# A decode kernel's last 30 microseconds: reordered tail products, residual accumulated in PSUM, and a different way of storing the result

## The chip, the cores and the metric

One core of one Trainium2 chip. The metric is the device time of one execution in microseconds (us); in this study the fast runs of one kernel on one chip lay at most 0.17% apart (front_longer, 661.01 to 662.14). The kernel before took 660.36 us (median of 3 runs, 660.25 to 660.48). The span of a profile is about 1.3 us shorter than the time of the same run.

## The reference, cut to what matters

A decoder block for one new token and two batch rows: layer norm, attention over a cache of 8192 positions with 32 heads, output product, residual, a second layer norm, a gated ReLU network, residual.

```python
x = A_x                                            # [2, 1, 512]
h  = x + attention(layernorm(x), k_cache, v_cache, wq, wo)   # caches [2, 32, 8192, 128] bf16
n  = layernorm(h)
h2 = h + (relu(n @ W_gate) * (n @ W_up)) @ W_down  # 512 -> 1376 -> 512
```

The caches are 2 x 134 MB, read once. The result is 2 x 512 bf16 values, 2 KB.

## The kernel before

The kernel streams K and V tiles of 4 MB through four SBUF slots. For each of 32 pairs of heads, VectorE computes three quarters of the scores, TensorE one quarter ("K part"), ScalarE the exponentials, TensorE the V product. The last two pairs, P0 and P1, are written out after the loop. The product with `wo` is spread: most of it (`L463`, 30 matmuls) can be done as soon as the third-last pair's result is gathered. This is TensorE's order at the end:

```python
k_part(tail, P0, (2, 3, 4, 5), ((k2p, 1),))          # scores of P0
nc.tensor.wait_ge(l2p, 1)
o_gather(tail)
nc.tensor.wait_ge(a2p, 7)                            # ScalarE copied the gathered O_all
nc.tensor.wait_ge(sem_wo, 16)
for r in range(DR):                                  # "wo product", 30 matmuls in four column tiles
    i = nc.tensor.matmul(Op[1][32 * (r % 4):32 * (r % 4) + B, :], lhsT=O_all[:, r, :], rhs=X[:, r * D:(r + 1) * D], ...)
tail.mark("op", i)
nc.tensor.wait_ge(a2p, 9)                            # ScalarE copied it to os_sb
for c in range(DC):                                  # "little product into W", fp32
    nc.tensor.matmul(Wp[:, c * B:(c + 1) * B], lhsT=os_sb[:]..., rhs=sel2[:], ...)
k_part(tail, P1, (10, 11, 12, 13), ((k2p, 2),))      # scores of P1
pv(tail, P0, ...)                                    # V product of P0
pv(tail, P1, ((V_LAST, J, (sem_vl[0] ...)), (0, V_LAST, (sem_vl[1] ...))), ...)   # of P1, by two loads
```

After that: `O_cur` (the last pair normalised), its product with wo, `hb` (the residual h), the mean, `d_b` (h minus its mean), the up and gate products, `hd` (their gated product), the down product. The down product is accumulated in four column tiles of one PSUM bank: columns 128m to 128m+127 of the result stand on partitions 32m and 32m+1. The ending before:

```python
for m in range(4):
    i = nc.tensor.matmul(Op[0][32 * m:32 * m + B, 0:128], lhsT=hd[0:kp, f * B:(f + 1) * B], rhs=wdn_block[:, 128 * m:128 * m + 128], ...)
t_y = pe.run(i)
dve.last()
dve.wait(t_y)
t = dve.run(nc.vector.scalar_tensor_tensor(          # one operation on 128 partitions: y * r2 + h
    out=o_r, in0=Op[0][:, 0:128], scalar=r2[:, 0:1], in1=h_r, op0=ALU.mult, op1=ALU.add))
sp.wait(t); act.wait(t)
for b, e in enumerate((nc.sync, nc.scalar)):         # four rows of 256 bytes each, from partitions b, b+32, b+64, b+96
    e.dma_start(out[b, 0].rearrange("(k n) -> k n", n=128), o_r[b:128:32, :]).then_inc(sem_out, 16)
nc.sync.wait_ge(sem_out, 16 * B)
```

The softmax here doesn't subtract the row's maximum and nothing guards it: scores larger than these inputs give would overflow.

## Time and profile before

| what | before |
|---|---|
| time | 660.36 us |
| span of the profiled run | 659.2 us |
| read from HBM | 281 MB at 426 GB/s over the span |
| last V tile landed, its two loads | 643.40 and 645.88 us |
| W_gate landed | 652.51 us |
| last rows of W_down landed | 656.06 us |
| last matmul ends | 656.70 us |
| stores issued, last store landed | 657.23, 659.14 us |

The landings are the moments at which a load's semaphore gets its last increment in the trace.

From the page of the kernel before: the rows by slice (40 slices of 16.5 us; a digit is tenths of DMA or clock, where PEclk is the granted clock, the share of TensorE's full speed that the chip allowed), and the line of the chain of waits by engine (the work that ended last, followed back from the end).

```profile
PEclk9856556565756657555665756756555765655656
DMA  8999999999999999999999999999999999999997
GB/s 366 444 437 431 420 445 416 443 428 431 438 422 441 422 439 433 428 435 424 441 422 439 433 428 433 426 441 422 439 434 426 435 424 441 424 437 433 428 417 295
...
DMA 76%; DVE 19%; PE 4%; issue 1%; ACT 1%; SPq 0%; DVEq 0%
```

The DMA engines are busy for 90% or more (digit 9) from the second slice to the last but one, so the kernel is a stream of 281 MB with a start and an end. How a landing is read: the issue of the last load, from SyncE's row of the timeline (start, length), and its line in the DMA issues of the page, which ends with the time from issue to landing:

```profile
628.22 2.39 SPq L706 DMA_DIRECT2D wd_last<-in_B_W_down_dram  x1
...
wd_last<-in_B_W_down_dram SPq DMA_DIRECT2D x1, 96.0 KB, 27.8
```

628.22 + 27.8 gives 656.0 us. Most of the chain's 4% of TensorE (some 26 us) lies before that, from 628 us on, beside the last loads. The timeline of the kernel before, from the wo product on; columns are start, busy time, engine, line, operation, in brackets the idle time before it and its releaser; SPq and ACTq are the DMA queues of SyncE and ScalarE, on which a store is issued:

```profile
628.78 3.58 PE L463 MATMUL O<-X,O_all 128*2 128x512 bf16 x30 [0.33 <-ACT O_all L671]
632.40 0.60 ACT L677 ACTIVATE os_sb<-O 128x512 f32<-128x512 f32 x1 [2.89 <-PE O L463]
633.05 2.03 PE L469 MATMUL W<-sel,os_sb 128*128 128x2 f32 x8 [0.69 <-ACT os_sb L677]
641.05 6.08 PE L405 MATMUL O<-slot,e 128*16 128x512 bf16 x56
647.38 0.61 PE L405 MATMUL O<-slot,e 128*16 128x512 bf16 x8
649.86 0.16 DVE L510 TENSOR_TENSOR O_cur<-Ob,zi 128x4 bf16<-128x4 f32 x1 [1.99 <-PE Ob L417]
653.29 1.72 PE L756 MATMUL O<-d_b,slot 128*128 128x2 bf16 x44
656.38 0.32 PE L808 MATMUL O<-wd_last,hd 96*2 96x128 bf16 x4
656.85 0.35 DVE L815 SCALAR_TENSOR_TENSOR kT<-O,r,kT 128x128 bf16<-128x128 f32 x1 [1.27 <-PE O L808]
657.22 0.65 SPq L820 DMA_DIRECT2D out_dram<-kT  x1
657.23 0.61 ACTq L820 DMA_DIRECT2D out_dram<-kT  x1
```

No V product and no gate product waits for a DMA here: V's last part starts at 647.38 us, 1.5 us after its data. In this trace compute is a little behind the stream. The chain of waits (start, us, what; "issue" is time for which the profile shows no wait) says the same: its end is compute, one exchange after the other.

```profile
655.36 1.37 PE O L808 x23
656.74 0.03 issue
656.76 0.02 DVEq L32
656.78 0.06 issue
656.85 0.35 DVE kT L815
```

### The profile page before, as it was taken

What the parts mean: (1) busy time and instruction counts of PE and PEld (TensorE: products, weight loads), DVE (VectorE), ACT (ScalarE), POOL (GpSimd) and SP (SyncE); (2) the same over time, 40 slices, a digit from 0 to 9 for tenths busy, and PEclk for the clock granted to TensorE, in tenths of its full rate; (3) what the DMA queues carried; (4) which work ended last, traced back from release to release, by engine and by line L of the source; (5) the groups of instructions that cost most, each with busy time, mean ns of one, the idle gap of its engine ahead of it and who ended that gap; (6) DMA issues with size and microseconds to landing.
All of it is one profiled execution on the core that took longest, in us unless ns stands there. A gap on an engine that the chain in (4) does not pass through costs nothing.

```text
span 659.2 us, 7582 instructions
## 1 busy us (share of the span) xinstructions
PE 324.3 (49%) x3073; PEld 188.6 (29%) x3073; DVE 469.2 (71%) x280; ACT 213.6 (32%) x431; POOL 73.5 (11%) x125
## 2 busy tenths in 40 slices
PE   2753454435455343655535364443556444354577
PEld 0331332213233121433313142221324222133344
DVE  1585576788767678776768877676886767787991
ACT  1622333143342223334223343422324332333250
POOL 3002002020200202020020201002020110202000
PEclk9856556565756657555665756756555765655656
DMA  8999999999999999999999999999999999999997
GB/s 366 444 437 431 420 445 416 443 428 431 438 422 441 422 439 433 428 435 424 441 422 439 433 428 433 426 441 422 439 434 426 435 424 441 424 437 433 428 417 295
DMA packets 10653, 281.17 MB, mean 427 GB/s; under 512 B 1202, under 2 KB 1300, under 8 KB 1812
## 3 DMA queue, kind: packets, MB, share of 16 engines
q1 hardware_dynamic: 10632, 281.06, 99.3%
q8 instruction: 5, 0.08, 0.1%
q14 instruction: 4, 0.03, 0.0%
q10 hardware_dynamic: 12, 0.00, 0.0%
HBM read 281.05 MB, written 0.00 MB: 426 GB/s over the span
## 4 chain that ended last, share of the span: by engine, by line
DMA 76%; DVE 19%; PE 4%; issue 1%; ACT 1%; SPq 0%; DVEq 0%
DMA slot<-in_A_k_cache_dram 76%; DVE prod L540 16%; DVE prod L549 2%; PE O L405 1%; PE O L463 1%; PE T L381 0%; ACT kT L566 0%; PE W L469 0%; DVE scores L554 0%; PE S L756 0%; PE O L756 0%; PE O L808 0%; PE Ob L417 0%; SPq L172 0%; PE S L364 0%
## 5 line engine op out<-in xcount | busy, mean ns | idle before, releaser
L540 DVE TENSOR_TENSOR prod<-slot,q_c 128x12288 bf16<-128x12288 bf16 x32 | 209.9, 6558 | 148.0 <-DMA slot<-in_A_k_cache_dram 141.3
L405 PE MATMUL O<-slot,e 128*16 128x512 bf16 x1024 | 119.3, 621 | 219.9 <-ACT e L495 146.2
L549 DVE TENSOR_TENSOR prod<-prod 128x6144 bf16<-128x6144 bf16 (+3 forms) x128 | 212.2, 1657 | 7.8
L566 ACT ACTIVATE kT<-T 128x1024 bf16<-128x1024 bf16 x128 | 126.1, 1022 | 144.6 <-PE T L381 141.9
L381 PE MATMUL T<-ident_f,slot 128*128 128x128 f32 x512 | 108.6, 365 | 29.1 <-DVEq L587 29.1
L405 PEld LDWEIGHTS O<-slot,e 128*16 128x16 bf16 x1024 | 26.4, 114 | 287.0 <-ACT e L495 172.9
L495 ACT ACTIVATE e<-scores 64x96 bf16<-64x96 f32 x64 | 19.5, 304 | 239.6 <-DVEq L601 238.9
L381 PEld LDWEIGHTS T<-ident_f,slot 128*128 128x128 f32 x512 | 79.0, 188 | 44.2 <-DVEq L587 43.3
L537 POOL COPY q_c<-q_all 128x136 bf16<-128x136 bf16 x32 | 57.2, 1788 | 195.5 <-DVEq L591 152.5
L364 PE MATMUL S<-q_c,kT 128*128 128x4 bf16 x1024 | 47.4, 168 | 40.8 <-ACT kT L566 40.0
L364 PEld LDWEIGHTS S<-q_c,kT 128*128 128x128 bf16 x1024 | 39.1, 104 | 67.9 <-ACT kT L566 66.8
L417 PE MATMUL Ob<-sel,os_sb 128*128 128x4 f32 x136 | 30.1, 345 | 24.2 <-ACT os_sb L569 24.2
L417 PEld LDWEIGHTS Ob<-sel,os_sb 128*128 128x128 f32 x136 | 28.6, 311 | 26.1 <-ACT os_sb L569 26.1
L520 POOL MEMSET O_l<- 128x40 bf16 (+1 forms) x13 | 1.8, 136 | 303.9 <-DVEq L598 303.9
L554 DVE TENSOR_REDUCE scores<-prod 128x96 f32<-128x768 bf16 x32 | 30.5, 953 | 2.8
L566 ACT ACT_TABLE_LOAD x15 | 19.2, 1283 | 0.3
L495 ACT ACTIVATE e<-S 64x32 bf16<-64x32 f32 x64 | 13.0, 202 | 15.1 <-PE S L364 14.7
L569 ACT ACTIVATE os_sb<-O 128x512 f32<-128x512 f32 x17 | 10.1, 597 | 12.8 <-PE O L405 12.4
L495 ACT ACTIVATION_READ_ACCUMULATOR e<-S 64x1 f32 x64 | 12.8, 201 | 0.7
L495 ACT ACTIVATION_READ_ACCUMULATOR e<-scores 64x1 f32 x64 | 11.8, 185 | 0.0
L426 PEld LDWEIGHTS Ob<-zs,ones_f 128*128 128x128 f32 x30 | 7.1, 296 | 12.5 <-issue 12.5
L525 POOL COPY rsel<-rows 128x30 bf16<-128x30 bf16 x28 | 5.9, 209 | 33.3 <-DVEq L598 32.5
(104 smaller groups left out, 90.6 us busy)
## 6 DMA issues: line engine op xcount, KB each, us to landing
slot<-in_A_k_cache_dram SPq DMA_DIRECT2D x32, 4096.0 KB, 32.1
slot<-in_A_v_cache_dram SPq DMA_DIRECT2D x31, 4096.0 KB, 30.3
slot<-in_A_wq_dram SPq DMA_DIRECT2D x1, 4096.0 KB, 12.2
X<-in_A_wo_dram SPq DMA_DIRECT2D x1, 3840.0 KB, 45.8
slot<-in_A_v_cache_dram SPq DMA_DIRECT2D x1, 3072.0 KB, 23.3
slot<-in_B_W_up_dram SPq DMA_DIRECT2D x1, 1376.0 KB, 23.2
slot<-in_B_W_gate_dram SPq DMA_DIRECT2D x1, 1376.0 KB, 26.2
slot<-in_A_v_cache_dram SPq DMA_DIRECT2D x1, 1024.0 KB, 25.4
```

Of the source, the lines that this page charges most:

```text
L364: i = nc.tensor.matmul(Sp[p % 2][:, 2 * jj:2 * jj + 4], lhsT=kv_[:, k, r, :], rhs=q_c[p % 2][:, 4 * r:4 * r + 4], start=(r == 0), stop=(r ...
L381: i = nc.tensor.transpose(Tp[g % 2][:, k * 128:(k + 1) * 128], k_t[:, j:j + 2, :].rearrange("p j d -> p (j d)").bitcast(F32), ident_f[:])
L405: i = nc.tensor.matmul(Op[0][c:c + 16, :], lhsT=e_t[q][:, j // VJ, :], rhs=v_t[:, j:j + VJ, :].rearrange("p j d -> p (j d)"), start=(q == ...
L417: i = nc.tensor.matmul(Ob[:, 0:4], lhsT=os_sb[:, jj * Dh:(jj + 1) * Dh], rhs=sel[:, 4 * jj:4 * jj + 4], start=(jj == 0), stop=(jj == VJ - 1))
L426: return nc.tensor.matmul(bank[:, ZC:ZC + 8], lhsT=ones_f[:], rhs=zs[:], start=True, stop=True)
L495: i = nc.scalar.activation(out=e_t[q][h, j0 // VJ:j1 // VJ, 8 * q:8 * q + 8].rearrange("p g (j a) -> p g j a", a=2)[:, :, :, a], in_=src(h ...
L537: nc.gpsimd.tensor_copy(out=q_c[p % 2][:], in_=q_all[:, p]).then_inc(g2d, 1)
L540: return nc.vector.tensor_tensor(out=prod[:, 0:JC, :], in0=tile((2 * p) % 4)[:, 0:JC, :], in1=q_c[p % 2][:, 8:QW].unsqueeze(1).broadcast_t ...
L549: run(nc.vector.tensor_tensor(out=prod[:, 0:JC, 0:w], in0=prod[:, 0:JC, 0:w], in1=prod[:, 0:JC, w:2 * w], op=ALU.add))
L554: return nc.vector.tensor_reduce(out=scores[p % PG][:, 0:JC], in_=prod[:, 0:JC, 0:8], axis=AX.X, op=ALU.add)
L566: to_pe(nc.scalar.activation(out=kT[gg % 2][:], in_=Tp[gg % 2][:].bitcast(BF16), func=ACT.Copy))
L569: to_pe(nc.scalar.activation(out=os_sb[:], in_=Op[0][:], func=ACT.Copy))
```

## The change

In a few words: the last product stays in four column tiles; VectorE and ScalarE copy two tiles each to two neighbouring partitions; two stores of 512-byte rows. The diff does more than that. It (a) puts the last K part before the wo product and the little product into W between the two V products; (b) accumulates the residual on TensorE and moves the layer norm's reciprocal to the up branch, so that nothing but copies remains at the end; and (c) changes copies and stores. The core of it:

```diff
@@ (a) TensorE's order; ScalarE's order follows it
                 k_part(tail, P0, (2, 3, 4, 5), ((k2p, 1),))
+                k_part(tail, P1, (7, 8, 9, 10), ((k2p, 2),))
                 nc.tensor.wait_ge(l2p, 1)
                 o_gather(tail)
                 ... wo product ...
                 tail.mark("op", i)
-                nc.tensor.wait_ge(a2p, 9)
+                pv(tail, P0, ((JC, J, ((slot_sem[1], 16),)), (0, JC, ((a2p, 13),))))
+                nc.tensor.wait_ge(a2p, 14)
                 ... little product into W ...
-                k_part(tail, P1, (10, 11, 12, 13), ((k2p, 2),))
-                pv(tail, P0, ((JC, J, ((slot_sem[1], 16), (a2p, 6))), (0, JC, ((a2p, 8),))))
                 pv(tail, P1, ...)
@@ (b) residual into the down product's bank; variance before gate; scale on u
-                        i = nc.tensor.matmul(
-                            Tp[0][32 * k:32 * k + B, c:128:DC], lhsT=hb[...], rhs=ident[...], start=True, stop=True)
+                        nc.tensor.matmul(
+                            Op[0][32 * k:32 * k + B, c:128:DC], lhsT=hb[...], rhs=ident[...],
+                            start=(c == 0), stop=False, skip_group_check=True)
+                for k in range(2):
+                    i = nc.tensor.matmul(Sp[0][:, 32:32 + B], lhsT=onesn[:], rhs=vh[:, k * B:(k + 1) * B], ...)
                 t_g = ffn_in(Op[1], wgt, 0, FC)
-                dve.run(nc.vector.tensor_copy(out=u_sb[:], in_=Sp[1][:, 0:FC * B]))
-                dve.run(nc.vector.tensor_copy(out=h_r, in_=Tp[0][:, 0:128]))
+                dve.run(nc.vector.tensor_tensor(out=u_sb..., in0=Sp[1]..., in1=r2... , op=ALU.mult))
@@ (c) the ending
-                dve.last()
-                t = dve.run(nc.vector.scalar_tensor_tensor(
-                    out=o_r, in0=Op[0][:, 0:128], scalar=r2[:, 0:1], in1=h_r, op0=ALU.mult, op1=ALU.add))
-                for b, e in enumerate((nc.sync, nc.scalar)):
-                    e.dma_start(out[b, 0].rearrange("(k n) -> k n", n=128), o_r[b:128:32, :])...
+                for m in range(2):
+                    dve.run(nc.vector.tensor_copy(out=o_r[:, 128 * m:128 * m + 128], in_=Op[0][32 * m:32 * m + B, 0:128]))
+                for m in range(2, 4):
+                    act.run(nc.scalar.activation(out=o_r[:, 128 * m:128 * m + 128], in_=Op[0][32 * m:32 * m + B, 0:128], func=ACT.Copy))
+                for m, (e, r) in enumerate(((sp, dve), (act, act))):
+                    e.wait((r.sem, r.count))
+                    e.eng.dma_start(out[:, 0, 256 * m:256 * m + 256], o_r[:, 256 * m:256 * m + 256])...
```

`o_r` is now two neighbouring partitions of 512 columns.

More of the change, by code (lines that the diff above doesn't have):

```diff
@@ L141, in bass_sequential_preLN__gqa_block_cached__glu_gated_reglu__decode_kernel @@
         vr = sb("vr", [128, B], F32)
-        ve = sb("ve", [128, 1], F32)
-        r2 = sb("r2", [128, 1], F32)
-        h_r = kT[0][:].bitcast(F32)[:, 0:128]
-        o_r = kT[1][:, 0:128]
+        ve = sb("ve", [128, B], F32)
+        r2 = sb("r2", [128, B], F32)
+        o_r = kT[1][0:B, 0:D]
         vh = sb("vh", [128, 2 * B], BF16)
@@ L457, in program @@
                 k_part(tail, P0, (2, 3, 4, 5), ((k2p, 1),))
+                k_part(tail, P1, (7, 8, 9, 10), ((k2p, 2),))
                 nc.tensor.wait_ge(l2p, 1)
                 o_gather(tail)
-                nc.tensor.wait_ge(a2p, 7)
+                nc.tensor.wait_ge(a2p, 12)
                 nc.tensor.wait_ge(sem_wo, 16)
@@ L669, in program @@
                         evacs()
+                    elif p == P1:
+                        evacs()
                         act.wait(tok("og", NI))
@@ L673, in program @@
                             in_=Op[1][:, 0:B * DR].rearrange("p (b r) -> p b r", r=DR), func=ACT.Copy))
-                        act.wait(t_s[p])
-                        exp_dve(p)
+                        act.wait(t_s[P0])
+                        exp_dve(P0)
                         act.wait(tok("op", NI))
                         to_pe(nc.scalar.activation(out=os_sb[:], in_=Op[1][:], func=ACT.Copy))
-                    elif p == P1:
-                        evacs()
                         act.wait(t_s[p])
@@ L766, in program @@
                     for c in range(DC):
-                        i = nc.tensor.matmul(
-                            Tp[0][32 * k:32 * k + B, c:128:DC], lhsT=hb[:, c * B:(c + 1) * B],
-                            rhs=ident[:, 32 * k:32 * k + 32], start=True, stop=True)
-                t_hr = pe.run(i)
-                pe.wait((sem_w[1], 16))
-                t_g = ffn_in(Op[1], wgt, 0, FC)
+                        nc.tensor.matmul(
+                            Op[0][32 * k:32 * k + B, c:128:DC], lhsT=hb[:, c * B:(c + 1) * B],
+                            rhs=ident[:, 32 * k:32 * k + 32], start=(c == 0), stop=False, skip_group_check=True)
                 dve.last()
@@ L782, in program @@
                 t_vh = dve.run(nc.vector.tensor_tensor(out=vh[:, B:], in0=vr[:], in1=vh[:, 0:B], op=ALU.subtract))
+                pe.wait(t_vh)
+                for k in range(2):
+                    i = nc.tensor.matmul(Sp[0][:, 32:32 + B], lhsT=onesn[:], rhs=vh[:, k * B:(k + 1) * B],
+                                         start=(k == 0), stop=(k == 1))
+                t_var = pe.run(i)
+                pe.wait((sem_w[1], 16))
+                t_g = ffn_in(Op[1], wgt, 0, FC)
+                dve.wait(t_var)
+                dve.run(nc.vector.tensor_scalar_add(out=ve[:], in0=Sp[0][:, 32:32 + B], scalar1=eps))
+                dve.last()
+                dve.run(nc.vector.reciprocal(out=r2[:], in_=ve[:]))
+                dve.last()
                 dve.wait(t_u)
-                dve.run(nc.vector.tensor_copy(out=u_sb[:], in_=Sp[1][:, 0:FC * B]))
-                dve.wait(t_hr)
-                dve.run(nc.vector.tensor_copy(out=h_r, in_=Tp[0][:, 0:128]))
+                dve.run(nc.vector.tensor_tensor(
+                    out=u_sb[:].rearrange("p (f b) -> p f b", b=B),
+                    in0=Sp[1][:, 0:FC * B].rearrange("p (f b) -> p f b", b=B),
+                    in1=r2[:].unsqueeze(1).broadcast_to([128, FC, B]), op=ALU.mult))
                 dve.last()
@@ L791, in program @@
                     in1=u_sb[:], op0=ALU.max, op1=ALU.mult))
-                pe.wait(t_vh)
-                for m in range(4):
-                    for k in range(2):
-                        i = nc.tensor.matmul(Sp[0][32 * m:32 * m + B, 32:33], lhsT=vh[:, k * B:(k + 1) * B],
-                                             rhs=onesn[:, 0:1], start=(k == 0), stop=(k == 1))
-                t_var = pe.run(i)
-                dve.wait(t_var)
-                dve.run(nc.vector.tensor_scalar_add(out=ve[:], in0=Sp[0][:, 32:33], scalar1=eps))
-                dve.last()
-                dve.run(nc.vector.reciprocal(out=r2[:], in_=ve[:]))
                 pe.wait(t_hd)
@@ L810, in program @@
                             rhs=(wdn[:, f, :] if f < 10 else wd_last[:])[:, 128 * m:128 * m + 128],
-                            start=(n == 0), stop=(n == FC - 1))
+                            start=False, stop=(n == FC - 1), skip_group_check=True)
                 t_y = pe.run(i)
-                dve.last()
                 dve.wait(t_y)
-                t = dve.run(nc.vector.scalar_tensor_tensor(
-                    out=o_r, in0=Op[0][:, 0:128], scalar=r2[:, 0:1], in1=h_r, op0=ALU.mult, op1=ALU.add))
-                sp.wait(t)
-                act.wait(t)
-                for b, e in enumerate((nc.sync, nc.scalar)):
-                    e.dma_start(
-                        out[b, 0].rearrange("(k n) -> k n", n=128), o_r[b:128:32, :]).then_inc(sem_out, 16)
+                act.wait(t_y)
+                for m in range(2):
+                    dve.run(nc.vector.tensor_copy(
+                        out=o_r[:, 128 * m:128 * m + 128], in_=Op[0][32 * m:32 * m + B, 0:128]))
+                for m in range(2, 4):
+                    act.run(nc.scalar.activation(
+                        out=o_r[:, 128 * m:128 * m + 128], in_=Op[0][32 * m:32 * m + B, 0:128], func=ACT.Copy))
+                for m, (e, r) in enumerate(((sp, dve), (act, act))):
+                    e.wait((r.sem, r.count))
+                    e.eng.dma_start(out[:, 0, 256 * m:256 * m + 256], o_r[:, 256 * m:256 * m + 256]).then_inc(sem_out, 16)
                 nc.sync.wait_ge(sem_out, 16 * B)
```

## The prediction

> **What bounds it now.** The DMA engines. The page's slices show 417 to 445 GB/s from the second to the last but one; 281 MB pass in a span of 659.2 us. The chain of waits is 76% DMA, all cache loads. The loads queue without a gap to the end. Landings by the trace (issue plus time to landing): last V tile 643.40 and 645.88 us, W_up 649.19, W_gate 652.51, W_down blocks 653.78, 655.08, 655.86, its last rows 656.06. Only 3.1 us come after the last input byte. All that the diff moves runs after 620 us.
>
> **What the diff does**, more than its title says:
>
> (a) From 628 us TensorE does the last K part (6.0 us) before, not after, the product with wo (3.6); the little product into W (2.0) goes between the two last V products (3.4 and 2.6 until the z sum). Nothing is removed. TensorE is the chain here by the timeline: from 628.1 to 647.0 it has 18 us of matmuls and 0.95 us of gaps for two ScalarE copies. In the new order: K part 628.05 to 634.1; the gathered copy waits behind the two exponentials of that K part (0.85 us), so wo runs 635.3 to 638.9; V to 642.3; W to 644.4; scores and V tile are there at 643.4; last V to 647.0. The same end within 0.2 us: a gap for a gap.
>
> (b) The layer norm's reciprocal goes onto the up branch, the residual is accumulated on TensorE. The variance matmuls (0.2 us, hidden so far behind the wait for hd) now stand between up and gate, two instead of eight: +0.1 us on the chain. VectorE is done with scaling about 654.1, before gate ends at 655.1.
>
> (c) Tail. One VectorE operation of 0.35 us (128x128 from PSUM) becomes two copies on VectorE and two on ScalarE. A 128-column copy took VectorE 0.29 us; two overlapping: estimate 0.43. ScalarE took 0.20 us for 32 columns, 0.60 for 512: estimate 0.28 for 128, 0.57 for two. Fewer partitions save nothing: columns set the time. So ScalarE's store is issued 0.2 us later. Stores: now two of four 256-byte packets. [...] Here a 256-byte packet takes 15 ns; the 1.9 us from issue to last landing are 1.25 to 1.5 until the first packet and 0.35 of receipt. So 512-byte rows save at most 0.1 us.
>
> **Sum.** (a) 0.0, (b) +0.1, (c) +0.2 less at most 0.1: +0.2 us on 660.36. A gain is capped: the last W_down rows land at 656.06, where the down product ends at 656.74 now, so (a) and (b) could give 0.6 us at most.
>
> Predicted 660.6 us, range 659.6 to 661.8. Faster by over 2%: 0.005; within: 0.985; slower: 0.01.
>
> **What would show it.** Landings unmoved within 0.2 us. TensorE starting its last stretch at 628 us and O_cur normalised at 649.9 within 0.3; order K, wo, V, W, V. Gate ending about 655.1, down about 656.8. ScalarE copies of 0.28 us, VectorE copies of 0.2 to 0.3; the ScalarE store issued about 657.6; last landing about 659.3.
>
> **What would make it wrong.** The granted clock: 0.5 nearly throughout the end, with one full grant at 646.9 to 650.4 us, under which the eight fp32 matmuls of the collection take 1.07 us; at half clock they took 1.87. If the new order moves that grant, the end moves by up to 1 us either way. Also a ScalarE table load before the new copies (1.28 us), which I don't expect.

The sum is 0.0 + 0.1 + 0.2 - 0.1 = +0.2 us. The -0.1 is the author's estimate, and the trace of the kernel before bounds it: the data packets of a store take 15 to 16 ns each, the first ones begin 1.25 and 1.51 us after the issues, and from a queue's first packet to the end of its last it is 0.07 and 0.08 us, so fewer packets can save no more than that if the time before the first stays. "Receipt" is the stretch from the last packet to the last landing (0.32 us from its end at 658.82 to 659.14). That fewer partitions save nothing was not shown by a trace at that time; the runs show it for a copy of 128 columns on VectorE: 0.29 us on 128 partitions (old_store), 0.28 on two (the changed kernel). The table loads of the kernel before, 1283 ns in the mean, all lie before 575 us, and the changed kernel has none before its new copies either.

## The result, and the profile after

The changed kernel took 660.12 us (median of 6 runs, 659.90 to 660.32) beside 660.34 us of the kernel before (6 runs, 660.09 to 660.49). The ratio is 0.9996, with a 95% interval of 0.9984 to 1.0009: the same, within 2% and within the noise of the ratio. (A ratio is the mean time of one kernel's fast runs over that of the other's of the same rounds, so it is not quite the ratio of the medians quoted.) Five more rounds on another chip gave 659.96 beside 660.52 us, ratio 0.9992 (0.9979 to 1.0006). So the medians were 0.2 and 0.6 us apart. The ratios alone do not show a gain; the traces below do, step by step.

The same timeline of the changed kernel:

```profile
636.01 3.41 PE L463 MATMUL O<-X,O_all 128*2 128x512 bf16 x30 [1.09 <-ACT O_all L672]
638.96 2.19 PE L404 MATMUL O<-slot,e 128*16 128x512 bf16 x32
641.08 2.03 PE L470 MATMUL W<-sel,os_sb 128*128 128x2 f32 x8
643.55 1.47 PE L404 MATMUL O<-slot,e 128*16 128x512 bf16 x24 [0.45 <-DMA slot<-in_A_v_cache_dram]
646.13 0.61 PE L404 MATMUL O<-slot,e 128*16 128x512 bf16 x8 [0.78 <-DMA slot<-in_A_v_cache_dram]
648.60 0.16 DVE L509 TENSOR_TENSOR O_cur<-Ob,zi 128x4 bf16<-128x4 f32 x1 [2.84 <-PE Ob L416]
652.68 1.72 PE L755 MATMUL O<-d_b,slot 128*128 128x2 bf16 x44 [0.45 <-DMA slot<-in_B_W_gate_dram]
656.34 0.28 PE L807 MATMUL O<-wd_last,hd 96*2 96x128 bf16 x4
656.67 0.57 ACT L818 ACTIVATE kT<-O 2x128 bf16<-2x128 f32 x2 [9.29 <-PE O L807]
656.67 0.59 DVE L815 CAST kT<-O 2x128 bf16<-2x128 f32 x2 [1.97 <-PE O L807]
657.27 0.26 ACTq L822 DMA_DIRECT2D out_dram<-kT  x1
657.29 0.31 SPq L822 DMA_DIRECT2D out_dram<-kT  x1
```

The last load, in the same two views of the changed kernel:

```profile
630.22 0.50 SPq L705 DMA_DIRECT2D wd_last<-in_B_W_down_dram  x1
...
wd_last<-in_B_W_down_dram SPq DMA_DIRECT2D x1, 96.0 KB, 26.1
```

It was issued 2 us later and landed at 656.3 us all the same, since it stands at the end of a queue that keeps the engines busy (the DMA row has a 9 to the last slice but one in both traces). Three things differ in the timeline. O_cur comes 1.26 us earlier (648.60 against 649.86). That lead is gone by the end: both V parts and the gate product now wait for their data, and the last matmul ends at 656.62 us where it ended at 656.70. And the ending has other pieces: two copies one after the other on each engine (0.57 and 0.59 us in all), and stores whose issue takes 0.26 and 0.31 us instead of 0.61 and 0.65.

The chain of waits now ends with the landing of the last W_down block, then the work that follows it:

```profile
629.40 26.68 DMA slot<-in_B_W_down_dram
656.09 0.04 issue
656.13 0.52 PE O L807 x7
656.65 0.02 issue
656.67 0.28 DVE kT L815
656.95 0.03 issue
656.98 0.28 DVE kT L815
```

The stores themselves are seen in the waits of SyncE's queue, the line for its wait on the stores' semaphore (total us, times, longest). First the kernel before:

```profile
SPq L822 <- DMA out_dram<-kT: 1.3, 1, 1.3
```

and the changed kernel:

```profile
SPq L823 <- DMA out_dram<-kT: 1.0, 1, 1.0
```

This wait starts when the issue is over. With the issue time added, a store takes 1.9 us before and 1.3 us after. The span splits as follows, up to rounding, by the records of the two traces:

| stretch | before | after | difference |
|---|---|---|---|
| start to last W_down landing | 656.06 | 656.29 | +0.23 |
| last landing to end of the last matmul | 0.64 | 0.33 | -0.31 |
| last matmul to issue of the later store | 0.52 | 0.67 | +0.15 |
| issue to last landing of the stores | 1.92 | 1.28 | -0.63 |
| landing to end | 0.03 | 0.03 | 0.00 |
| span | 659.17 | 658.61 | -0.56 |

The first row is the stream's own variation: over all full-size traces the last W_down landing lay between 655.99 and 656.36 us, with no order to it. The third row has two parts: the copies take 0.59 us where one operation took 0.35, but they start 0.05 us after the last matmul where it started after 0.15. The diff also drops a wait of VectorE before it (`dve.last()`, which the chain before shows as DVEq L32). The other rows are the subject of the experiments.

### The profile page after: what moved, and what is told of

It reads as the page before. It is cut to its first block, busy times and chain, and to the rows that moved or that the text cites. A ratio compares the mean times of both kernels' runs of the same rounds, so it can differ in the third digit from the quotient of the medians.

```text
span 658.6 us, 7569 instructions
## 1 busy us (share of the span) xinstructions
PE 326.1 (50%) x3066; PEld 192.1 (29%) x3067; DVE 469.4 (71%) x280; ACT 214.2 (33%) x433; POOL 72.7 (11%) x125
## 4 chain that ended last, share of the span: by engine, by line
DMA 80%; DVE 18%; issue 1%; SPq 0%; DVEq 0%; PE 0%
DMA slot<-in_A_k_cache_dram 76%; DVE prod L539 16%; DMA slot<-in_B_W_down_dram 4%; DVE prod L548 2%; DVE scores L553 0%; SPq L171 0%; SPq L702 0%; SPq L698 0%; DVE kT L815 0%; DVEq L586 0%; PE O L807 0%; DVEq L590 0%; SPq L175 0%; SPq L174 0%; DVE zi L505 0%
## 5 line engine op out<-in xcount | busy, mean ns | idle before, releaser
L404 PE MATMUL O<-slot,e 128*16 128x512 bf16 x1024 | 117.2, 609 | 219.3 <-ACT e L494 146.3
L380 PE MATMUL T<-ident_f,slot 128*128 128x128 f32 x512 | 112.8, 376 | 29.4 <-DVEq L586 29.4
L380 PEld LDWEIGHTS T<-ident_f,slot 128*128 128x128 f32 x512 | 81.9, 193 | 44.4 <-DVEq L586 43.6
L565 ACT ACT_TABLE_LOAD x15 | 19.2, 1283 | 0.3
```

What stands on the lines that cost most here:

```text
L380: i = nc.tensor.transpose(Tp[g % 2][:, k * 128:(k + 1) * 128], k_t[:, j:j + 2, :].rearrange("p j d -> p (j d)").bitcast(F32), ident_f[:])
L404: i = nc.tensor.matmul(Op[0][c:c + 16, :], lhsT=e_t[q][:, j // VJ, :], rhs=v_t[:, j:j + VJ, :].rearrange("p j d -> p (j d)"), start=(q == ...
L565: to_pe(nc.scalar.activation(out=kT[gg % 2][:], in_=Tp[gg % 2][:].bitcast(BF16), func=ACT.Copy))
```

## The experiments

Twelve kernels ran, in three groups; each group shared its own runs of the kernel before. Times are medians. "Matmul to end" is the end of the last matmul to the end of the span, "issue to landing" that of the later store, both from the trace.

The theory after the result was: the ending (c) gives the gain, the order (a) brings the front forward but the landings hold it back. The rival was that the order gives the gain.

### after_again: the changed kernel once more, no edit

> The changed kernel once more, as the control for its chip. Every theory: 0.2 to 0.3 us under the kernel before. Theory G (the gain of 0.2 us is the ending: the stores save 0.6 us from issue to landing, the copies cost 0.25): the down product's last matmul to the end of the span takes 1.9 to 2.0 us whatever the granted clock does, and the last W_down landing is at 656.0 to 656.4. Rival H (the new order gains, the front is earlier by 1.2 us): O_cur normalised at 648.6 again. If the front's 1.2 us came from the granted clock instead, it lies anywhere between 648.5 and 650 and moves with the clock records of 630 to 650 us.

Measured: 659.96 us beside 660.52. Matmul to end 1.98 us, last landing 656.01, O_cur 648.44. The ending repeats to 0.01 us. O_cur also repeats, so this run by itself does not tell order from clock.

### old_store: the changed kernel with the old copy and the old stores

```diff
-                for m in range(2): ... dve copies ...; for m in range(2, 4): ... act copies ...
-                ... two stores of two 512-byte rows ...
+                t = dve.run(nc.vector.tensor_copy(out=o_w, in_=Op[0][:, 0:128]))        # 128x128
+                for b, e in enumerate((nc.sync, nc.scalar)):
+                    e.dma_start(out[b, 0].rearrange("(k n) -> k n", n=128), o_w[b:128:32, :])...
```

> The changed kernel with the ending before: one VectorE copy of 128x128 from PSUM, two stores of four 256-byte rows from four partitions each. Theory G: copy 0.29 us in place of 0.60, each store's issue 0.6 us long again, first packet 1.25 us after issue, last landing 1.9 us after it; from the last matmul to the end 2.3 us, so 0.3 us over the changed kernel and equal to the kernel before. Rival H (the order gives the gain): stays 0.2 us under the kernel before.

Measured: 660.06 us (changed kernel 659.96, before 660.52, same chip). The copy:

```profile
656.58 0.29 DVE L814 CAST kT<-O 128x128 bf16<-128x128 f32 x1 [1.79 <-PE O L808]
```

Issue to landing 1.84 us, matmul to end 2.25 us, which is 0.26 us over the changed kernel, as theory G expected of the trace. The expected time, "equal to the kernel before", was missed: it lay 0.1 us over the changed kernel. The single copy here is 0.29 us faster up to the issue than the changed kernel's four (0.38 against 0.67), and the stores lose 0.56 us. Against the kernel before, the store is issued 0.14 us sooner (0.38 against 0.52): the old ending on top of (b) has a lighter operation (0.29 us for 0.35) and no `dve.last()`. So the new stores and copies by themselves are worth 0.26 us in the trace, and some of the shorter ending comes with (b).

### split_rows: the changed kernel, each 512-byte row as two pieces of 256

```diff
-        o_r = kT[1][0:B, 0:D]
+        o_p = kT[1][0:B, 0:640].rearrange("p (m n) -> p m n", n=160)[:, :, 0:128]      # gaps between the pieces
...
+                    e.eng.dma_start(out[:, 0, 256 * m:256 * m + 256].rearrange("b (k n) -> b k n", n=128),
+                                    o_p[:, 2 * m:2 * m + 2, :])...
```

> The changed kernel with each 512-byte row of a store cut into two pieces of 256 bytes (padded apart in SBUF), still from two partitions. If the size of the rows under 512 bytes or the number of packets makes the store slow (rival R): issue to last landing about 1.9 us, as before. If the spread over four partitions does (theory P): about 1.3 us, as in the changed kernel. The time differs from the changed kernel by +0.6 us under R, 0 under P.

Measured: 659.71 us, issue to landing 1.29 us, matmul to end 1.99 us. The trace has eight packets of 256 bytes, as the kernel before has, of 15 to 18 ns each, where the changed kernel has four of 512 bytes, of 27 to 32 ns. Rival R falls: neither the row size nor the number of packets made the old store slow. The issue lines of this run:

```profile
657.11 0.27 ACTq L822 DMA_DIRECT2D out_dram<-kT  x1
657.14 0.32 SPq L822 DMA_DIRECT2D out_dram<-kT  x1
```

### four_adjacent and two_strided: number of partitions, or their distance?

Both give a wrong result: they store from the wrong partitions. Both start from old_store.

```diff
 # four_adjacent: four 256-byte rows per store, from neighbouring partitions
-    o_w[b:128:32, :]
+    o_w[4 * b:4 * b + 4, :]
 # two_strided: two 512-byte rows per store, from partitions b and b + 32
-    out[b, 0].rearrange("(k n) -> k n", n=128), o_w[b:128:32, :]
+    out[b, 0].rearrange("(k n) -> k n", n=256), o_w[b:64:32, :]        # o_w now 256 columns wide
```

> Ending as in old_store, but the four 256-byte rows of each store come from four neighbouring partitions, not from every 32nd (wrong result on purpose). If the distance of 32 partitions makes the store's issue long (theory N): issue 0.3 us, last landing 1.3 us after issue. If the number of partitions, four against two, does (theory M): issue 0.6 us, landing 1.8 to 1.9 us.

> Ending as in old_store, but each store takes two 512-byte rows from two partitions 32 apart (wrong result on purpose: half of each row is old data). Theory N: issue 0.6 us, landing 1.8 to 1.9 us after it. Theory M: issue 0.3, landing 1.3.

Measured, one look each: four_adjacent 1.33 us from issue to landing, two_strided 1.87 us. The issue lines, first four_adjacent:

```profile
656.68 0.32 SPq L818 DMA_DIRECT2D out_dram<-kT  x1
656.69 0.28 ACTq L818 DMA_DIRECT2D out_dram<-kT  x1
```

then two_strided:

```profile
657.05 0.63 SPq L818 DMA_DIRECT2D out_dram<-kT  x1
657.05 0.60 ACTq L818 DMA_DIRECT2D out_dram<-kT  x1
```

Theory N holds and M falls: it is the distance of 32 partitions, not the count, that doubles the issue (0.28 to 0.32 us against 0.60 to 0.63). The first packet follows it: 0.73 to 0.76 us after the first issue with neighbouring partitions, 1.23 to 1.25 with partitions 32 apart. Four rows of 256 bytes from neighbouring partitions are nearly as quick as two of 512 (1.33 against 1.28 us). Only distances of 1 and 32 were tried; whether 2 or 16 would do the same, and why the distance costs time, stays open.

### one_store: one store of two 1024-byte rows

```diff
-                for m, (e, r) in enumerate(((sp, dve), (act, act))): ... two stores ...
+                sp.wait((dve.sem, dve.count), (act.sem, act.count))
+                nc.sync.dma_start(out[:, 0, :], o_r).then_inc(sem_out, 16)
+                nc.sync.wait_ge(sem_out, 16)
```

> The changed kernel with one store on SyncE alone, two rows of 1024 bytes. If two stores issued at the same time hold each other up (rival Q): issue to last landing 1.2 us or less, 0.1 to 0.2 us shorter than with two. If each store's cost is its own (theory P): 1.3 us, no difference in time.

Measured: 659.72 us (659.46 to 659.99) beside 659.96 of the changed kernel and 660.52 of the kernel before; correct. Issue to landing 1.14 us, matmul to end 1.86 us. With two stores the landings come in two pairs 0.17 to 0.18 us apart (658.38/658.39 and 658.56/658.58 in the changed kernel); with one store there is one pair. Rival Q is right about the size, 0.14 us; that the rows of one store are also longer (1024 bytes) was not tested apart. This is the best correct version found; its lead over the changed kernel is seen in the trace, and the ratio (0.9989, 0.9976 to 1.0003) does not resolve it.

### order_only and old_order: the order (a) alone, and everything but the order

order_only is the kernel before with hunk (a); old_order is the changed kernel with hunk (a) taken back:

```diff
 # order_only = before +
+                k_part(tail, P1, (7, 8, 9, 10), ((k2p, 2),))        # ahead of o_gather; pv(P0) ahead of W
 # old_order = after -
-                k_part(tail, P1, (7, 8, 9, 10), ((k2p, 2),))        # as in the kernel before
```

> The kernel before with the new order of the last K part, the wo product and the V products alone; its own layer norm and ending. Theory G: the time of the kernel before within 0.15 us, since the landings of W_gate and W_down (652.5 and 656.1) hold the rest up however early the front is. Rival H: 0.2 us faster or more.

> The changed kernel with the old order back (last K part after the wo product). Theory G: the changed kernel's time within 0.15 us, so 0.2 to 0.3 us under the kernel before. Rival H: the time of the kernel before. O_cur normalised at 649.9 us if the clock is 0.5 up to 646.9, earlier with more full clock.

Measured: order_only 660.27 us, old_order 659.87, both beside 660.31. So the order alone moved the median by -0.04 us (ratio 1.0001) and the change without the order by -0.44 us (ratio 0.9995). In the medians rival H falls and theory G holds, but old_order came out further under the kernel before than G's 0.2 to 0.3 us; again no interval excludes 1. In the traces, O_cur came at 649.25 us with the new order and at 650.17 without, but matmul to end was 2.47 and 1.99 us. In the profiled run of old_order (660.21 us, the second slowest of its five) the last matmul ended 0.92 us after the last landing, so a late front can still cost 0.6 us in a single execution.

### less_v: 1 MB less to load

```diff
-                        for k, (j0, j1) in enumerate(((V_LAST, J), (0, V_LAST))):
+                        for k, (j0, j1) in enumerate(((V_LAST, J),)):
...
-                pv(tail, P1, (..., (0, V_LAST, ((a2p, 15), (sem_vl[1], 16)))),
+                pv(tail, P1, (..., (0, V_LAST, ((a2p, 15),))),
```

The tile then holds the V rows of an earlier pair in that part; that changes the numbers a little, and the comparison with the reference still passed.

> The changed kernel without the load of the second piece of the last V tile (1 MB, 2.4 us of the DMA stream); wrong result on purpose, the tile holds older V rows there. All later landings come 2.4 us earlier. If the DMA landings alone set the end (rival D): 2.4 us faster. Theory T (DMA and the compute chain are nearly tied): the compute chain takes over at once, and the gain is only its slack, 0 to 1.0 us, depending on the granted clock.

Measured: 657.81 us, 2.50 under the kernel before; old_order, with the same ending on the same chip, was 0.44 under it, so the missing megabyte gave about 2.1 us. That is near rival D's 2.4 and outside theory T's 0 to 1.0. T had overlooked that the front itself waits for V: without the second piece, that part of the V product starts at 645.27 instead of 646.13 us and O_cur comes at 647.75. Then compute takes over: the gate product no longer waits, and the last matmul ends 0.88 us after the last landing (653.72), against 0.33. So compute in the new order had about 2 us in hand over the whole stretch, not 1.

### front_longer: 2 us more on TensorE

```diff
+                for c in range(DC):                  # the little product once more, into unused columns
+                    nc.tensor.matmul(Op[1][:, c * B:(c + 1) * B], lhsT=os_sb..., rhs=sel2[:], start=True, stop=True, ...)
                 pv(tail, P1, ...)
```

> The changed kernel with the eight fp32 matmuls of the little product into W done twice (the second time into unused columns): 1.0 us more on TensorE's front at full clock, 2.0 at half. Rival D: no difference. If the front were wholly on the chain: +1 to +2 us. Theory T: the slack is used up first, +0.3 to +1.4 us.

Measured: 661.39 us (661.01 to 662.14), 1.08 over the kernel before and 1.5 over old_order. The added matmuls took 2.0 us (started at 643.02); O_cur came at 650.92, the last matmul ended 1.56 us after the last landing. Theory T's range is met only at its upper edge, or just missed, for the changed kernel itself did not run on this chip: part of the added time vanishes in the waits, the rest shows. Two things make the trace less clean. The added matmuls took 2.0 us at full clock, where 1.0 was expected; the timelines above already show 2.03 us for this product at half clock (before) and at full clock (after). And the clock fell to half at 646.0 us, where it stayed full to 649.4 in the changed kernel's trace. The last V part started only 1.07 us later than there; the rest of the 2.32 us by which O_cur is late came after, with that V part taking 1.03 us for 0.61 and the product behind it (into Ob) 1.87 for 1.05.

### w_later and before_again: is the early front the order or the clock?

w_later is the kernel before with one move; before_again is the kernel before, unchanged.

```diff
+                k_part(tail, P1, (10, 11, 12, 13), ((k2p, 2),))
                 nc.tensor.wait_ge(a2p, 9)
                 ... little product into W ...
-                k_part(tail, P1, (10, 11, 12, 13), ((k2p, 2),))
```

> The kernel before with one move: the little product into W after the last K part instead of before it; the K part still follows the wo product. Theory E (the new order gains because independent matmuls follow the wo product, so its drain of 0.65 us and the 0.65 us ScalarE copy behind it are no longer waited for): the K part's transposes start 2.9 to 3.0 us after the wo product's first matmul, where before it was 6.0 to 6.3 with the W product between; O_cur at 648.9 to 649.4; the last matmul ends 0.3 to 0.4 us after the last W_down landing, where before it was 0.64. Rival C (the granted clock alone made the front early): O_cur at 649.8 to 650.2 unless full clock lies before 646 us. Time 0.0 to 0.3 us under the kernel before.

> The kernel before once more, for a second trace of its end. Theory E: O_cur at 649.8 to 650.3 whatever the clock, as the last K part cannot start before 634.9; last matmul 0.6 to 0.9 us after the last W_down landing; from there to the end 2.47 us.

Earlier traces show theory E's two times: in order_only the next product began 2.95 us after the wo product's first matmul, while that was busy for 3.58, so 0.63 us of it were no longer waited for (the "drain"); ScalarE's copy took 0.60 us in the kernel before.

Measured: w_later 660.34 us beside 660.41 (ratio 0.9998). Its transposes started 3.50 us after the wo product's first matmul, not 2.9 to 3.0, but far earlier than before (6.2). O_cur came at 649.68, outside both theories' ranges, with full clock from 636.3 to 639.7 and 646.5 to 649.9 us. This run settles nothing about the clock.

before_again contradicts theory E in its strong form: O_cur at 648.60, as early as with the new order, and the last matmul 0.33 us after the last landing. The clock records of that run have full speed from 644.0 to 650.8 us. Its 56 V matmuls, with the same work as in the kernel before's first trace:

```profile
641.17 4.57 PE L405 MATMUL O<-slot,e 128*16 128x512 bf16 x56
646.13 0.61 PE L405 MATMUL O<-slot,e 128*16 128x512 bf16 x8
652.67 1.73 PE L756 MATMUL O<-d_b,slot 128*128 128x2 bf16 x44 [0.59 <-DMA slot<-in_B_W_gate_dram]
```

4.57 us against 6.08. So the old order also meets the landings when it gets the clock. What stays open is whether the order influences when the clock is granted; grants were seen in different places in every trace (the last full one from 646.9 to 650.4 us in the kernel before, 639.1 to 649.4 in the changed kernel).

### The endings of all traces together

| traces | rows per store | partitions | matmul to issue | issue to landing | matmul to end |
|---|---|---|---|---|---|
| before, before_again, w_later, order_only | 4 x 256 B | 32 apart | 0.52 | 1.83 to 1.92 | 2.39 to 2.47 |
| old_store | 4 x 256 B | 32 apart | 0.38 | 1.84 | 2.25 |
| two_strided | 2 x 512 B | 32 apart | 0.37 | 1.87 | 2.27 |
| after, after_again, old_order, less_v, front_longer | 2 x 512 B | neighbours | 0.67 to 0.68 | 1.26 to 1.28 | 1.97 to 1.99 |
| split_rows | 4 x 256 B | neighbours | 0.67 | 1.29 | 1.99 |
| four_adjacent (wrong result) | 4 x 256 B | neighbours | 0.37 | 1.33 | 1.74 |
| one_store | one store, 2 x 1024 B | neighbours | 0.69 | 1.14 | 1.86 |

## Why the prediction was right, and where it was not

The time was inside the range (659.6 to 661.8) and the class, within 2%, was right. The sign of the small number was not: 0.2 us slower was forecast, the medians came out 0.2 and 0.6 us faster.

- **The hit itself says little.** A range of 2.2 us on an ending of 2.5 us, and a class 13 us wide on either side, were hard to miss once the landings were known to stay. The sum inside it was wrong by 0.5 us.
- **What bounds it: right.** The landings stayed where they were (within 0.23 us), less_v moved the end by about 2.1 us per megabyte, and the cap of "0.6 us at most" for (a) and (b) is what stopped the 1.26 us of the front. Last landing to last matmul went from 0.64 to 0.33 us, and in the eight full-size traces with the new order, unburdened, it was 0.32 or 0.33 every time. With the old order it was 0.64, 0.92, 0.33 and 0.32.
- **(a) "a gap for a gap": the sum was near, the reasoning was off.** order_only shows the time unmoved. But I counted the wo product as 3.6 us of TensorE. In the new order the V product starts 2.95 us after the wo product's first matmul (order_only: 635.36 and 638.31, at half clock), because it does not need the result; the last 0.6 us and ScalarE's 0.6 us copy behind it are hidden. (Not every product can do this: the transposes of w_later, which do not need the result either, began only after 3.50 us.) So the last V product could start at 643.60 instead of the 644.4 of my sum, at once after its data. In time this was worth nothing measurable, for the landings of V, W_gate and W_down come in between.
- **(b) +0.1 us: not seen.** From O_cur to hd it took 5.24, 5.28 and 5.31 us in the three traces with hunk (b) and no wait for W_gate (old_order, less_v, front_longer), and 5.27 in the kernel before. The granted clock differed between them (old_order had full clock to 652.9 us, the kernel before to 650.4), so a tenth cannot be told apart here. In the other traces with the change the stretch contains a DMA wait.
- **(c), the failing step: "512-byte rows save at most 0.1 us".** The stores saved 0.63 us in the first pair of traces, 0.56 us between old_store and after_again. I had seen that the time of a store lies before the first packet and took it to be fixed. It is not: with partitions 32 apart the issue takes 0.60 to 0.65 us and the first packet comes after about 1.25 us, with neighbours 0.26 to 0.32 and about 0.73. And the rows' size, which the title of the change and my argument both looked at, shows no part in it (split_rows, two_strided). That larger rows save anything was my assumption; the runs do not show it: 1.29 us with 256-byte rows (split_rows), 1.28 with 512 (the changed kernel).
- **(c), the copies: direction right, the size partly by luck.** Two ScalarE copies 0.57 us, as forecast; two VectorE copies 0.59, where I had 0.43 from an assumed overlap, such as the trace before has between two smaller operations (L789 and L799: starts 655.13 and 655.23, the first 0.18 us long). They started 0.31 us apart with 0.28 us each, so they did not overlap. "Columns set the time" held: 0.29 us on 128 partitions (old_store), 0.28 on two. Up to the issue the change costs 0.15 us; the forecast was 0.2. It came near because the dropped wait, which the sum did not have, gave back 0.10 us of the 0.24 that the copies added.
- **The clock: rightly named as the risk.** It moved the front of the same kernel by 1.26 us between two traces (649.86 and 648.60, before and before_again), and the end by about 0.3.

With the measured terms in place of mine, the ending gives +0.15 and -0.63 us, the rest is capped: about 0.5 us less, more if the front happens to be late before. The medians, -0.22 and -0.56, agree within the noise of the runs. The medians cannot share the gain out among (a), (b) and (c): old_store, with the old stores, was 0.46 us under the kernel before on its chip, old_order 0.44 and order_only 0.04 on theirs, and every one of these intervals contains 1.

## What to carry to other kernels

In a kernel that streams from HBM to its last microseconds, look up when the last input lands and count forward from there: here what followed that moment stayed shortened (0.48 us in the traces), and of the 1.26 us gained ahead of it all but 0.31 were given back at the landings. When a tiny store ends the kernel, look at the partitions it reads: gathering the rows on neighbouring partitions paid here (0.56 us from issue to landing) although the copies cost 0.29 us more than a single one, and one store for all of it was faster than two at once (1.14 against 1.28 us). When costing an order of matmuls, ask whether the next one needs the result; here the wo product was busy for 3.58 us, and an independent V product began after 2.95, independent transposes after 3.50.
